# q loaded four tokens to a row, head halves on partition halves, in a retention and mixture-of-depths kernel

## Chip, cores and metric

The kernel runs on one core of one Trainium2 chip. The metric is the device time of one execution in microseconds: the median of several runs for the comparison, and one profiled run for the trace. The span of a trace is a little shorter than the time of a run (116.6 us of span in a profiled run of 118.38 us).

## What is computed

Two stages, the second on the output of the first. The reference, cut to what matters:

```python
# q, k, v: (4, 8, 768, 64) float32; x: (4, 768, 512)
def _attn_ref(q, k, v):
    gamma = 1.0 - 2.0 ** (-5.0 - np.arange(H))
    for t in range(S):
        state = gamma * state + einsum('bhd,bhe->bhde', k[:, :, t], v[:, :, t])
        y[:, :, t] = (1 / sqrt(D)) * einsum('bhd,bhde->bhe', q[:, :, t], state)

def _moe_ref(x, w_gate, w1, w2, capacity):          # x = y with the heads side by side
    scores = einsum('bsd,d->bs', x, w_gate)
    out = x.copy()
    for b in range(B):
        top_idx = argpartition(-scores[b], capacity)[:capacity]      # capacity = 128 of 768
        xe = x[b, top_idx]
        ye = maximum(xe @ w1, 0) @ w2                # 512 -> 1024 -> 512
        out[b, top_idx] = xe + sigmoid(scores[b, top_idx])[:, None] * ye
```

The kernel does the first stage in chunks. There are 12 tiles `j` (4 batches, 3 tiles of 256 tokens each). In a tile, the decay is put into q and k as factors (`gq`, `gk`), the products of q and k are masked and multiplied with v, and the state of all earlier tokens is added. The second stage needs the scores of all 768 tokens of a batch before it can rank them.

## The kernel before

All work is written as small functions, and a long string `ORDER` names them in the order in which they are put on the engines. Each engine takes its own instructions in that order. The names that the text uses: `l_q`, `l_k`, `l_v` load half a tile (j, half u), `l_wg` loads w_gate, `c_...` make constants, `warm` multiplies zeros, `cq` casts the first q tile, `ks` scales k, `tq` and `tk` transpose q and k on TensorE, `eq` and `ek` bring them to SBUF, `qk` and `mk` are the score product and its mask, `kv` and `se` add to the state and copy it, `qs` and `av` are the two products that make y, `ey`, `tx`, `ex` bring y to token order, `sp` and `esp` are the scores, `srt`, `esr`, `cp`, `cpi`, `dg`, `rk` rank them, `oh`, `gx`, `ga`, `gr` gather, `m1`, `rl`, `m2`, `cb` are the expert, `st` stores, and `sca` scatters.

The start of the order (cut):

```python
ORDER = (
    "c_tab;c_iota;l_k 0 1;c_zero;l_wg;c_small;l_q 0 1;l_q 0 0;l_k 0 0;l_v 0 0;c_mask;c_gq 0;l_v 0 1;c_ident;"
    "c_slg;c_szero;l_q 1 1;l_q 1 0;c_gk 1;l_k 1 1;cq 0 1;c_gq 1;c_wg;c_iota3;tq 0 1 S6;warm S0;l_k 1 0;l_v 1 0;"
    "eq 0 1 S6;warm S1;cq 0 0;c_gk 0;c_late;l_k 2 0;tq 0 0 S6;warm S2;l_v 1 1;c_gq 2;warm S3;l_k 2 1;ks 0 0;"
    "l_q 2 1;warm S4;eq 0 0 S6;ks 0 1;l_q 2 0;tk 0 0 S6;tq 1 2 S5;ek 0 0 S6;l_v 2 0;kv 0;eq 1 2 S5;tk 0 1 S6;"
    "l_k 4 1;qk 0 0 P0;ek 0 1 S6;mk 0 0 P0;l_v 3 0;se 0;qk 0 1 P1;..."
```

The functions that the change touches, and their neighbours:

```python
QX = many(NX, [128, H, 2, D], BF, "qx")     # NX = 7 buffers; KX and VX alike
QF = sb.tile([128, H, 2, D], FT)            # first q tile, float32; KF for k

def tok(src, j, u):                         # 128 rows of 2 tokens, 4 heads: 512 runs of 512 B
    b, jt = divmod(j, NJ)
    return bass.AP(tensor=src.tensor, offset=src.offset + b * H * S * D + jt * T * D + (u % 2) * 4 * S * D,
                   ap=[[2 * D, 128], [S * D, 8 if u == 2 else 4], [1, 2 * D]])

def load(x, src, j, u):                     # float32 in HBM, bf16 in SBUF
    h = slice(0, H) if u == 2 else slice(4 * u, 4 * u + 4)
    nc.gpsimd.dma_start(x[j % NX][:, h].rearrange("p h r d -> p h (r d)"), tok(src, j, u))

def l_q(j, u):
    if j:
        load(QX, q, j, u)
    else:
        nc.sync.dma_start(QF[:, 4 * u:4 * u + 4].rearrange("p h r d -> p h (r d)"), tok(q, j, u))

def l_wg():                                 # 512 elements of 4 B, one by one
    nc.sync.dma_start(wgf[:, :, 0], bass.AP(tensor=moe_w_gate.tensor, offset=moe_w_gate.offset,
                                            ap=[[1, 128], [128, HP]]))

def warm(bank):
    for _ in range(4):
        pe.matmul(PS[bank][:, :512], zero[:, :128], zero, start=True, stop=True)

def tq_(j, u, bank):
    for hp in range(HP)[hs(u)]:
        for r in range(2):
            for s in range(2):
                pe.transpose(tb(bank)[s * 64:(s + 1) * 64, hp, :, r, :], QX[j % NX][:, 2 * hp + s, r, :], ident)

def eq(j, u, bank):
    ve.tensor_mul(QT[j % 3][:, hs(u)]..., tb(bank)[:, hs(u)]..., gq[:, j % NJ, hs(u)]...)

def qk(j, u, bank):                         # weights: kT (64 x 64), moving: qT (64 x 128)
    for h in range(2):
        for r in range(2):
            for s in range(2):
                for c in range(2):
                    pe.matmul(p[c * 64:(c + 1) * 64, s, h, r, :], KT[...][...], QT[...][...], ...)

def ey(j, bank):                            # back to token order
    ac.activation(YT[j % 3].rearrange("p c h (i r) -> p (c h) i r", r=2),
                  PS[bank].rearrange("p (g r i) -> p g i r", g=2 * HP, r=2), AF.Copy)
```

## Time and profile before

| | before |
|---|---|
| time, median of 3 runs | 117.97 us (117.95 to 119.13) |
| span of the profiled run | 116.6 us |
| busy: TensorE (matmul), its weight loads | 93.6, 73.0 us |
| busy: DVE, ACT, POOL | 79.6, 73.5, 76.9 us |
| bytes moved by DMA | 19.69 MB in 44,003 packets |

The page gives the busy time of each engine, the span in 40 slices with a digit in tenths for each, the chain of work that ended last, the costliest groups of instructions, and the loads with the time from issue to landing. Some groups (engine, operation, out <- in, count, busy time and mean of one):

| group | count | busy us | mean ns |
|---|---|---|---|
| DVE mask `am <- pA, mask`, 128x1024 | 24 | 28.8 | 1219 |
| DVE `qT <- pA, gq`, 128x1024 | 10 | 6.9 | 685 |
| ACT `yT <- pA`, 128x1024 | 12 | 12.3 | 1022 |
| POOL issue of `vx`, `kx`, `qx` loads | 24, 22, 22 | 18.7, 17.5, 17.1 | 789, 799, 796 |
| TensorE transposes of q to `pA`, 128x128 out | 160 | 6.6 | 222 |

The mean of one TensorE instruction is its whole passage; instructions overlap, so the busy time of a group is far less than count times mean. A row of waits reads: who waited, for whom, microseconds in total, times, and the longest. A row of the stretches reads: from and to, length, then busy time and number of instructions of TensorE, its weight loads, DVE, ACT and POOL, then the granted clock, the share of the DMA engines (over 1 where packets overlap) and the GB/s written.

### The profile page before, as it was taken

What the parts mean: (1) busy time and instruction counts of PE and PEld (TensorE: products, weight loads), DVE (VectorE), ACT (ScalarE), POOL (GpSimd) and SP (SyncE); (2) the same over time, 40 slices, a digit from 0 to 9 for tenths busy, and PEclk for the clock granted to TensorE, in tenths of its full rate; (3) what the DMA queues carried; (4) which work ended last, traced back from release to release, by engine and by line L of the source; (5) the groups of instructions that cost most, each with busy time, mean ns of one, the idle gap of its engine ahead of it and who ended that gap; (6) DMA issues with size and microseconds to landing.
All of it is one profiled execution on the core that took longest, in us unless ns stands there. A gap on an engine that the chain in (4) does not pass through costs nothing.

```text
span 116.6 us, 4536 instructions
## 1 busy us (share of the span) xinstructions
PE 93.6 (80%) x1962; PEld 73.0 (63%) x1962; DVE 79.6 (68%) x218; ACT 73.5 (63%) x117; POOL 76.9 (66%) x129
## 2 busy tenths in 40 slices
PE   0089979998999888879988969898899999999000
PEld 0033557876777666669867757787789669884000
DVE  5295187983966999983794999969499795333000
ACT  7994279986698777836246949898687417143200
POOL 7999999989997998912999897870040060800800
PEclk9999999999999999985599999999999999999985
DMA  2999999999999999996999999999939007670270
GB/s 60 211 225 178 180 178 180 178 180 178 180 189 184 191 181 178 188 268 68 227 85 142 123 275 204 219 309 385 391 105 351 9 6 90 178 98 0 90 90 0
DMA packets 44003, 19.69 MB, mean 169 GB/s; under 512 B 36880, under 2 KB 39952, under 8 KB 43984
## 3 DMA queue, kind: packets, MB, share of 16 engines
q0 software_dynamic: 41344, 18.36, 114.5%
q1 hardware_dynamic: 2640, 1.05, 3.5%
q8 instruction: 15, 0.25, 0.8%
q14 instruction: 4, 0.03, 0.1%
HBM read 23.07 MB, written 7.34 MB: 261 GB/s over the span
## 4 chain that ended last, share of the span: by engine, by line
PE 62%; ACT 12%; issue 11%; DMA 6%; POOLq 2%; DVE 1%; POOL 1%; SPq 1%; ACTq 0%
PE pA L181 42%; PE pB L181 13%; PE pS L181 7%; ACT yT L181 4%; DMA QF<-in_q_dram 3%; ACT sst L181 3%; ACT kT L181 2%; DMA out_dram<-xs 2%; POOLq L645 2%; ACT xg L181 1%; POOL out_dram L595 1%; ACT xs L181 1%; DVE qT L181 1%; ACT ot L181 0%; SPq L277 0%
## 5 line engine op out<-in xcount | busy, mean ns | idle before, releaser
L181 DVE TENSOR_TENSOR am<-pA,mask 128x1024 bf16<-128x1024 f32 x24 | 28.8, 1219 | 3.7 <-PE pA L181 2.1
L589 POOL DMA_DIRECT2D out_dram<-xs x12 | 8.7, 722 | 16.4 <-ACT wr L181 8.2
L296 POOL DMA_DIRECT2D vx<-in_v_dram x24 | 18.7, 789 | 1.0 <-PE pA L181 0.5
L296 POOL DMA_DIRECT2D kx<-in_k_dram x22 | 17.5, 799 | 0.9 <-issue 0.3
L181 PEld LDWEIGHTS <-kp 64*128 64x128 bf16 (+1 forms) x256 | 14.9, 96 | 4.3 <-issue 0.8
L296 POOL DMA_DIRECT2D qx<-in_q_dram x22 | 17.1, 796 | 0.1
L181 ACT ACTIVATE sst<-pS 64x256 bf16<-64x256 f32 x40 | 15.0, 375 | 3.3 <-PE pS L181 2.5
L181 DVE TENSOR_SCALAR g<-wr,sc 128x256 bf16<-128x256 f32 (+4 forms) x44 | 15.9, 415 | 0.8 <-ACT wr L181 0.8
L181 ACT ACTIVATE yT<-pA 128x1024 bf16<-128x1024 f32 x12 | 12.3, 1022 | 4.7 <-PE pA L181 4.4
L595 POOL DMA_INDIRECT out_dram<-ot,idx x4 | 5.9, 1477 | 12.8 <-ACT ot L181 6.8
L181 PE MATMUL pS<-vx,kp 64*128 64x128 bf16 x160 | 12.3, 217 | 0.4 <-ACT sst L181 0.2
L181 PEld LDWEIGHTS <-qx 128*64 128x64 bf16 x192 | 6.0, 113 | 8.7 <-DVE qx L181 6.3
L181 PE MATMUL pA<-am,vx 64*64 64x128 bf16 x384 | 9.5, 220 | 2.1 <-issue 2.1
L181 PE MATMUL pA<-qT,kT 64*64 64x128 bf16 x384 | 9.8, 227 | 1.5 <-ACT kT L181 1.0
L181 ACT ACTIVATE kT<-pB 128x1024 bf16<-128x1024 bf16 (+1 forms) x8 | 7.3, 916 | 5.6 <-PE pB L181 5.5
L181 PEld LDWEIGHTS <-yT 128*128 128x128 bf16 x192 | 8.8, 99 | 3.1 <-ACT yT L181 2.4
L181 ACT ACTIVATE xs<-pA 128x1024 bf16<-128x1024 bf16 x10 | 10.2, 1022 | 0.9 <-PE pA L181 0.6
L181 DVE TENSOR_TENSOR qT<-pA,gq 128x1024 bf16<-128x1024 bf16 x10 | 6.9, 685 | 5.2 <-PE pA L181 5.2
L181 PEld LDWEIGHTS <-kT 64*64 64x64 bf16 x384 | 6.7, 110 | 3.7 <-ACT kT L181 2.0
L181 PEld LDWEIGHTS <-vx 64*64 64x64 bf16 x384 | 6.2, 106 | 3.8 <-issue 2.4
L181 DVE TENSOR_TENSOR kp<-kx,gk 128x512 bf16<-128x512 bf16 x22 | 8.3, 417 | 0.0
L181 PE MATMUL pA<-xg,w 128*128 128x128 bf16 x128 | 7.8, 219 | 0.0
(98 smaller groups left out, 172.0 us busy)
## 6 DMA issues: line engine op xcount, KB each, us to landing
out_dram<-xs POOLq DMA_DIRECT2D x12, 512.0 KB, 7.8
vx<-in_v_dram POOLq DMA_DIRECT2D x24, 128.0 KB, 5.4
qx<-in_q_dram POOLq DMA_DIRECT2D x22, 128.0 KB, 5.5
kx<-in_k_dram POOLq DMA_DIRECT2D x22, 128.0 KB, 5.6
w<-in_moe_w_dram POOLq DMA_DIRECT2D x8, 256.0 KB, 7.1
KF<-in_k_dram SPq DMA_DIRECT2D x2, 256.0 KB, 4.2
QF<-in_q_dram SPq DMA_DIRECT2D x2, 256.0 KB, 4.4
out_dram<-ot,idx POOLq DMA_INDIRECT x4, 4.8
```

The costliest lines, as they stand in the source:

```text
L181: i = getattr(self.engine, name)(*a, **k)
L296: nc.gpsimd.dma_start(x[j % NX][:, h].rearrange("p h r d -> p h (r d)"), tok(src, j, u))
L589: i = nc.gpsimd.dma_start(o, xs[:, 2 * j:2 * j + 2, :])
L595: i = nc.gpsimd.indirect_dma_start(out=out_rows, out_offset=bass.IndirectOffsetOnAxis(ap=IDX[b][:, :1], axis=0), in_=OT[b % 2], in_offset= ...
L645: with _tile.TileContext(nc) as tc:
```

## The change

Each q load now takes rows of four tokens (1 KB of float32, 512 B of bf16) instead of two. So that a load still covers four heads and 256 tokens, heads 0 to 3 lie on partitions 0 to 63 and heads 4 to 7 on partitions 64 to 127. A load has 256 runs instead of 512. The purpose is fewer and longer descriptors for q, to relieve the DMA queue and the engine that writes it. The queries of a tile then come out of the transposes in another order: (r, i) with token 4i + r, where it was 2i + r. The decay table, the mask and the copy back to token order follow that order. k and v keep two tokens to a row.

w_gate, 512 elements of 4 B each, goes to the end of the SyncE queue, behind k and q of the first tile; before it was second.

The order of all work was made anew for this: in particular the warm-up multiplications (16 instead of 20) stand ahead of all other TensorE work, the first state update follows them, and q of tile 0 is cast, transposed and evicted in one piece rather than two halves.

```diff
-    QX = many(NX, [128, H, 2, D], BF, "qx")
+    QX = many(NX, [128, 4, 4, D], BF, "qx")
-    QF = sb.tile([128, H, 2, D], FT)
+    QF = sb.tile([128, 4, 4, D], FT)
-    gq = sb.tile([128, NJ, HP, 2, 2, 64], BF)
+    gq = sb.tile([128, NJ, HP, 2, 4, 32], BF)
-    mask = sb.tile([128, 2, 2, 64], BF)
+    mask = sb.tile([128, 2, 4, 32], BF)
...
     def l_q(j, u):
-        if j:
-            load(QX, q, j, u)
-        else:
-            nc.sync.dma_start(QF[:, 4 * u:4 * u + 4].rearrange("p h r d -> p h (r d)"), tok(q, j, u))
+        o, jt = divmod(j, NJ)
+        src = bass.AP(tensor=q.tensor, offset=q.offset + o * H * S * D + jt * T * D + u * 4 * S * D,
+                      ap=[[4 * D, 64], [S * D, 4], [1, 4 * D]])
+        e, x = (nc.gpsimd, QX[j % NX]) if j else (nc.sync, QF)
+        e.dma_start(x[u * 64:(u + 1) * 64].rearrange("p h r d -> p h (r d)"), src)
...
-    def tq_(j, u, bank):
-        for hp in range(HP)[hs(u)]:
-            for r in range(2):
-                for s in range(2):
-                    pe.transpose(tb(bank)[s * 64:(s + 1) * 64, hp, :, r, :], QX[j % NX][:, 2 * hp + s, r, :], ident)
+    def tqb(bank):
+        return bf(bank).rearrange("p (u g c r i) -> p u g c r i", u=2, g=2, c=2, r=4)
+
+    def tq_(j, bank):
+        for h in range(4):
+            s = slice(h % 2 * 64, h % 2 * 64 + 64)
+            for r in range(4):
+                pe.transpose(tqb(bank)[s, :, h // 2, :, r, :], QX[j % NX][:, h, r, :], ident)
...
-    def eq(j, u, bank):
+    def eq(j, bank):
...
-      ... r=2),  PS[bank].rearrange("p (g r i) -> p g i r", g=2 * HP, r=2), AF.Copy)
+      ... r=4),  PS[bank].rearrange("p (g r i) -> p g i r", g=2 * HP, r=4), AF.Copy)
```

The start of the new order (the rest is cut; tiles 2 and 3 and tiles 8 and 9 overlap in other ways, and the order behind the last attention product differs in which expert comes first):

```diff
+    "c_small;c_tab;c_iota;l_k 0 0;l_q 0 1;l_k 0 1;l_v 0 0;c_slg;l_q 0 0;c_zero;c_szero;c_gk 0;l_q 1 1;warm S6;"
+    "c_ident;l_v 0 1;l_wg;c_gq 0;l_k 1 0;warm S6;l_k 1 1;l_v 1 0;c_gq 1;warm S6;c_iota3;ks 0 1;warm S6;l_q 1 0;"
+    "c_late;l_q 3 0;c_gq 2;l_k 2 1;l_v 1 1;ks 0 0;l_q 3 1;c_gk 1;cq 0;kv 0;l_q 2 1;c_wg;tq 0 S6;se 0;l_q 2 0;"
+    "tk 0 1 S0;tk 0 0 S1;l_k 2 0;ek 0 1 S0;eq 0 S6;ek 0 0 S1;l_k 3 0;ks 1 2;c_gk 2;qk 0 0 P1;l_v 2 1;c_mask;"
+    "qk 0 1 P2;tk 1 2 S6;mk 0 0 P1;l_v 2 0;tq 1 S0;ek 1 2 S6;l_k 3 1;mk 0 1 P2;qs 0 P1;kv 1;l_k 5 0;av 0 0 P1;..."
```

## The prediction

> **What bounds the kernel now.** I read the page first: busy times, the slices, the chain. From the slices, three lines, one digit for each 2.9 us:

> ```profile
> PE   0089979998999888879988969898899999999000
> ...
> PEclk9999999999999999985599999999999999999985
> DMA  2999999999999999996999999999939007670270
> ```

> TensorE is busy from about 6 us to 108 us, and DMA is full until about 60 us. The clock drops once in the middle (slices 18 to 20). The page's chain that ended last, by engine:

> ```profile
> PE 62%; ACT 12%; issue 11%; DMA 6%; POOLq 2%; DVE 1%; POOL 1%; SPq 1%; ACTq 0%
> ```

> So TensorE sets the end. Then the waits by engine, to see what TensorE still waits for and whether anybody waits for the loads that the change touches:

> ```profile
> PE pB L181 <- DVE qx L181: 6.3, 1, 6.3
> PE pA L181 <- issue: 3.4, 7, 0.9
> PE pA L181 <- ACT kT L181: 1.0, 2, 0.6
> DVE qx L181 <- DMA QF<-in_q_dram: 2.1, 1, 2.1
> ```

> The one long wait of TensorE is at the start, for the first q tile; its other waits for ACT and DVE add up to 3.7 us (ACT 1.0 + 0.9 + 0.8 + 0.6 + 0.2, DVE qT 0.2). After the first tile no compute engine waits for a transfer. The chain in order of time shows what the start is made of:

> ```profile
> 1.77 4.00 DMA QF<-in_q_dram
> ...
> 6.34 0.64 PE pB L181 x8
> 6.98 3.53 PE pA L181 x8
> 10.50 0.44 PE pB L181 x7
> 10.94 2.70 PE pA L181 x12
> ...
> 15.35 0.60 ACT kT L181
> ```

> The `pA` groups of 8 and 12 are the warm-up multiplications of zeros: 6.2 us of TensorE standing between the q transposes and the first k transposes. The first real score product (`qk 0`) starts at 15.24 us in the timeline, and by then only q of tiles 0 and 1, k of tile 0 and one state update are done. That stretch is where the new order can win. From there to `av 11`, the last attention product (88.8 us), the order is already dense; after it TensorE runs without a gap to 108 us.

> The last view is the GB/s row of the DMA answer for the first 12 us, 0.3 us per slice:

> ```profile
> GB/s 0 0 0 0 0 0 24 27 285 350 189 103 87 61 203 309 326 325 248 207 197 270 309 293 240 204 178 183 173 183 173 182 178 178 179 177 179 178 178 180
> ```

> The dip to 61 GB/s between 3.0 and 4.2 us is the w_gate transfer, 512 packets of 4 bytes, second in the SyncE queue. It landed 2.8 us after its issue at 1.23, so at 4.03.

> [...] Today every cast load of q, k and v writes 256 B rows (512 B read as fp32), and the trace has 36,880 of 44,003 packets under 512 B at a steady 178 to 180 GB/s written. The new q rows are 512 B. [...] the first eight warm-up multiplications take 3.59 us (0.45 each), the next twelve 2.76 us (0.23 each).

> **The change part by part.** *q loads, steady state.* 22 loads of 512 rows become 22 of 256. POOL's descriptor work goes by rows in the groups: 0.58 us for w1 (128 rows), 0.72 for w2 and stores (256), 0.79 for today's loads (512). I estimate 0.72 for the new ones, 22 x 0.07 = 1.5 us of POOL. It lies off the path: nobody waits for these loads. Worth 0 to 0.3 us.

> *Transposes and evictions.* A tile needs 16 q transposes before (4 pairs x 2 tokens x 2 heads) and after (4 head slots x 4 tokens), each 128x64 to 64x128. `eq` stays one 128x1024 multiply (0.68 us), `mk` 1.22 us, `ey` 1.02 us; only the order of columns within them changes. Sum 0. Four of 20 warm-up multiplications go.

> *w_gate behind the tile.* The dip is about (330 x 4 - 440) GB/s x 0.3 us = 264 KB, 0.8 us of first-tile traffic. q and k of tile 0 land up to 0.8 us earlier.

> *The start.* I replay it by hand with durations of the timeline. ACT first: table load and `first` end at 2.24; `gk 0` waits for `slg`, about 2.4, and takes 1.04 to 3.5; `gq 0`, `gq 1`, `gq 2` take 2.08 + 2.06 + 2.06 to 9.7; `gk 1` to 10.7; `se 0` 0.77 to 11.5; two half `ek 0` 0.60 each to 12.7. So `qk 0 0` starts near 12.8. DVE: constants to about 4; `ks 0 1` when its k lands (third in the queue, issued near 1.8, plus 3.1 to 4.0 us as the first k and the first q took), about 5.2 to 6.0; `c_late` 0.86 to about 7.1 (it waits for POOL's iota near 6.4); `ks 0 0` 0.75 to 7.9; `cq 0` about 1.0 to 1.4, to 9; `c_wg` 0.9, then `eq 0` 0.69 to 10.6, in time for 12.8. TensorE: 16 warm-ups from 3.0 (9 at 0.43, 7 at 0.22) to about 8.4; `kv 0`, `tq 0`, `tk 0` fit between 8.4 and 10.3. The first score product moves from 15.2 to 12.8, 2.4 us; the old order has then also transposed q of tile 1 (0.55), so the lead is about 1.9 us. Going on: `mk 0 0` 13.3 to 14.5, `mk 0 1` to 15.7, `av 0 1` done near 16.2 against 19.5 before (which has one more `kv`, 0.55: lead 2.75); `av 1` done near 20.3 against 24.0, where the old order is some 0.8 us of TensorE work further: lead near 2.8. At `qk 2` the same account gives about 2.5. I take **2.5 us**.

> *The rest.* The matmul work from there to the end is the same. In both lists what remains on TensorE behind `av 11` is the same sum: three expert first layers (about 1.95 each), four second layers (1.89 each), two rank sums (1.04 each), two gathers (1.50 each) and small ones, about 22 us. So the lead arrives at the end unless the new order waits more between. The old one has 3.7 us of dependency waits, and instruction gaps (0.3 to 0.9 us, no releaser) that should stay. I take 0 for the difference, plus or minus 1.5 us.

> Sum: 118.0 - 2.5 (start) - 0.2 (loads) + 0.5 (risk of a clock drop at the start, below) = 115.8; rounded for the gate's smaller share to **115.7 us**.

> **Rivals.** *The clock falls at the start.* After the warm-up the new order gives TensorE only some 1.7 us of work in 8.4 to 12.8. In the old trace 46 to 50 us, busy 3.20 of 4.00, was followed by this:

> ```profile
> 50.00:54.00 4.00, 3.45 (x86) 3.20 (x75) 2.21 (x9) 2.52 (x3) 0.00 (x0) 0.70 1.47 211
> 54.00:58.00 4.00, 4.00 (x60) 3.31 (x58) 2.91 (x5) 1.25 (x2) 3.04 (x6) 0.50 0.72 155
> ```

> The seventh figure is the clock. An emptier stretch may well do it again; tile 0 at half clock costs about 1 us, of which DVE's mask multiplications hide part. Time then 116.7. *The middle drop vanishes or comes twice.* TensorE does 60 instructions in 54 to 58 where 84 is usual, so a drop costs 2 to 3 us: 113.5 without, 118.5 with another. *ACT becomes the bound early.* It works from 2.4 to 20 us nearly without a pause in my replay, and one `ek` or `ey` behind an `se` moves everything: 116.5. *Loads arrive late.* The new order computes earlier from a queue that starts no earlier: `v 1 1` and `k 2 0` are issued near 9.3 and 12 and land some 5.4 us later (median of v), near 15 and 17.5; wanted near 19. Margin 2 us, unless 64-partition loads are slow. If they took 1.5 times as long, tiles 2 to 4 would wait and the time would be 119. The steady 0.73 us spacing against this. *The loads were the bound after all*, and fewer descriptors give more: [...] the waits speak against it.

> **Range and chances.** The start is worked out to about 1 us, the middle to 1.5 us, the clock to 1.5 us: together some 2.4 us for 8 in 10, a little more for the unreplayed 60 us in between. Range **112.5 to 118.8**. The 2% line lies at 115.6, almost on my number: faster by over 2% **0.47**, within **0.42**, slower by over 2% **0.11** (needs 120.3: late loads or two more clock drops).

> **What would show it.** Right: `qk 0` near 12.8 us, ACT being what it waits for; `av 11` near 86; the same gapless tail; no compute wait on q; POOL near 0.72 us per q load. Wrong: waits of DVE `kp` or TensorE on a transfer, a clock row with a drop near slice 4 or a second one later, dependency waits of TensorE well over 3.7 us, or a q transpose or `qT` eviction slower than 0.22 and 0.68 us.

## The result, and the profile after

In the first comparison the changed kernel takes 114.68 us (median of four runs, 113.19 to 117.55), the kernel before on the same chip 118.38 us (117.95 to 119.13). The ratio is 0.958, with a 95% interval of 0.950 to 0.966. Ratios leave disturbed executions out, and on this core few are left, so each is read beside the median of all executions.

One comparison is not enough here: executions of one and the same kernel differ by 3 to 6 us. The changed kernel was therefore measured twice more (e1 and e9 below). Over the three, its 14 executions have a mean of 115.57 us (two more on record for the first comparison, of 115.06 and 113.75 us, would make it 115.42), and 55 executions of the kernel before in the same comparisons 118.21 us: 2.6 us or 2.2% less. From the spread of these executions the difference is known to about 1.1 us either way, so that the kernel is faster is shown, and that it is so by over 2% is not: the interval of the first comparison is clear of 2%, those of e1 and e9 are not, and that of e1 includes 1. The prediction was 115.7 us from 118.0, 2.3 us less. Its range (112.5 to 118.8) held all three medians.

The profile after is of an execution of 115.92 us, span 114.1. Its slices (2.85 us each) and the chain by engine, from the page:

```profile
PE   0997799979898989795987979498999999999200
...
PEclk9999999999999999999679999976999999999965
DMA  2999999999999999999999999999206067520270
...
PE 47%; issue 16%; DVE 11%; ACT 8%; POOL 6%; DMA 5%; POOLq 2%; DVEq 0%; ACTq 0%
```

Two things differ from before. TensorE starts at 2.6 us, not 6.3. And the clock now drops twice (slices 20, 21 and 27, 28) where it dropped once; that execution is still faster. "issue", time in which an engine waited for nothing that the profile shows, has 16% of the chain where it had 11%.

Its first rows of the timeline of TensorE (start, length, what, and in brackets the idle time ahead with what ended it):

```profile
2.58 5.83 PE L181 MATMUL pB<-zero 128*128 128x512 bf16 x16 [2.58 <-DVE zero L248]
8.54 0.67 PE L181 MATMUL pS<-vx,kp 64*128 64x128 bf16 x4
9.75 0.38 PE L181 MATMUL pS<-vx,kp 64*128 64x128 bf16 x4 [0.54 <-DMA vx<-in_v_dram]
...
10.66 0.62 PE L181 MATMUL pA<-ident,kp 128*128 128x128 bf16 x8
12.23 0.64 PE L181 MATMUL pA<-qT,kT 64*64 64x128 bf16 x32 [0.95 <-ACT kT L181]
```

The first score product starts at 12.23 us (12.6 in e1's profile) against 15.24. The waits by engine, those of TensorE and the one long wait of a compute engine for a load:

```profile
DVE kp L181 <- DMA KF<-in_k_dram: 3.2, 1, 3.2
...
PE pB L181 <- DVE zero L248: 2.6, 1, 2.6
...
PE pA L181 <- issue: 2.5, 4, 1.4
...
PE pB L181 <- issue: 1.9, 2, 1.2
...
PE pA L181 <- ACT kT L181: 1.0, 1, 1.0
...
PE pS L181 <- DMA vx<-in_v_dram: 0.5, 1, 0.5
```

The 6.3 us that TensorE waited for the first q tile are gone. Its waits without a releaser ("issue") add up to 4.4 us where they were 3.9 (the 3.4 that the prediction shows and 0.5 for `pB`), and the longest is 1.4 us where it was 0.9. The chain in order of time says where they lie, and what the start hangs on now:

```profile
2.16 0.90 POOL vx L296
3.06 0.67 POOL qx L304
3.73 5.99 DMA vx<-in_v_dram
...
51.74 1.21 issue
...
71.42 1.44 issue
```

The first state update waits for v of tile 0, whose transfer takes 5.99 us; the chain goes over it, not over q. (In e9's profile it goes over k of tile 0, 5.28 us, instead.) The two gaps are followed by the two clock drops. The stretches of 4 us (busy time and instructions of TensorE, its weight loads, DVE, ACT and POOL, then clock, DMA share, GB/s written) show each gap and the drop behind it:

```profile
50.00:54.00 4.00, 2.79 (x85) 2.38 (x84) 3.03 (x7) 1.66 (x3) 3.62 (x6) 1.00 1.66 196
54.00:58.00 4.00, 4.00 (x52) 3.61 (x49) 4.00 (x8) 0.76 (x2) 3.48 (x7) 0.61 1.57 188
70.00:74.00 4.00, 2.56 (x66) 2.17 (x63) 2.63 (x7) 2.49 (x4) 2.68 (x5) 1.00 1.38 337
74.00:78.00 4.00, 4.00 (x74) 3.17 (x72) 2.96 (x4) 3.81 (x6) 1.55 (x4) 0.67 1.45 402
```

From the last attention product (ended 86.6 us, before 88.8) to the end of the span are 27.5 us, before 27.8: the tail is the same.

The GB/s row of the first 12 us after, 0.3 us for each slice:

```profile
GB/s 0 0 0 0 0 0 148 87 292 307 217 355 309 196 251 265 208 156 202 245 256 231 216 192 138 88 94 109 109 141 133 149 138 156 163 175 168 183 183 182
```

The dip of w_gate has moved from 3.0 to 4.2 us to 7.5 to 8.7 us, behind k and q of the first tile. Its lowest slice is 88 GB/s, where it was 61, with less traffic around it, and w_gate itself lands 5.9 us after its issue instead of 2.8.

### The profile page after: what moved, and what is told of

It reads as the page before. It is cut to its first block, busy times and chain, and to the rows that moved or that the text cites. A ratio compares the mean times of both kernels' runs of the same rounds, so it can differ in the third digit from the quotient of the medians.

```text
span 114.1 us, 4540 instructions
## 1 busy us (share of the span) xinstructions
PE 94.0 (82%) x1958; PEld 73.4 (64%) x1958; DVE 79.9 (70%) x216; ACT 74.0 (65%) x117; POOL 74.6 (65%) x128
## 2 busy tenths in 40 slices
DMA packets 37859, 19.69 MB, mean 172 GB/s; under 512 B 25616, under 2 KB 33808, under 8 KB 37840
## 4 chain that ended last, share of the span: by engine, by line
PE 47%; issue 16%; DVE 11%; ACT 8%; POOL 6%; DMA 5%; POOLq 2%; DVEq 0%; ACTq 0%
PE pA L181 27%; PE pB L181 11%; PE pS L181 9%; DMA vx<-in_v_dram 5%; DVE am L181 5%; POOL out_dram L598 4%; DVE g L181 3%; ACT kT L181 3%; DVE qT L181 2%; ACT xs L181 2%; POOLq L648 2%; ACT yT L181 1%; ACT ht L181 1%; POOL vx L296 1%; ACT sst L181 1%
## 5 line engine op out<-in xcount | busy, mean ns | idle before, releaser
L181 DVE TENSOR_TENSOR am<-pA,mask 128x1024 bf16<-128x1024 f32 x24 | 28.8, 1219 | 3.9 <-PE pA L181 2.9
L181 ACT ACTIVATE sst<-pS 64x256 bf16<-64x256 f32 x40 | 15.0, 375 | 9.4 <-PE pS L181 6.9
L181 PEld LDWEIGHTS <-kp 64*128 64x128 bf16 (+1 forms) x256 | 15.4, 98 | 6.4 <-issue 2.4
L296 POOL DMA_DIRECT2D kx<-in_k_dram x22 | 16.7, 765 | 1.7 <-DMA kx<-in_k_dram 0.8
L181 DVE TENSOR_SCALAR g<-wr,sc 128x256 bf16<-128x256 f32 (+4 forms) x44 | 16.6, 446 | 0.0
L304 POOL DMA_DIRECT2D qx<-in_q_dram x22 | 14.0, 637 | 2.0 <-DMA vx<-in_v_dram 0.8
L181 ACT ACTIVATE yT<-pA 128x1024 bf16<-128x1024 f32 x12 | 12.2, 1022 | 3.3 <-issue 1.8
L181 PE MATMUL pS<-vx,kp 64*128 64x128 bf16 x160 | 13.2, 221 | 1.0 <-DMA vx<-in_v_dram 0.5
L181 ACT ACTIVATE xs<-pA 128x1024 bf16<-128x1024 bf16 x9 | 9.2, 1024 | 4.3 <-PE pA L181 4.1
L181 PE MATMUL pA<-qT,kT 64*64 64x128 bf16 x384 | 9.5, 224 | 2.0 <-ACT kT L181 1.0
L181 PEld LDWEIGHTS <-yT 128*128 128x128 bf16 x192 | 8.7, 97 | 2.5 <-ACT yT L181 0.9
L181 PE MATMUL pA<-am,vx 64*64 64x128 bf16 x384 | 8.6, 224 | 0.9 <-issue 0.9
L181 PEld LDWEIGHTS <-kT 64*64 64x64 bf16 x384 | 6.4, 108 | 4.1 <-issue 1.8
L181 DVE TENSOR_TENSOR kp<-kx,gk 128x512 bf16<-128x512 bf16 x22 | 8.2, 419 | 0.1
L181 PE MATMUL pB<-zero 128*128 128x512 bf16 x16 | 5.8, 545 | 2.6 <-DVE zero L248 2.6
L181 PEld LDWEIGHTS <-vx 64*64 64x64 bf16 x384 | 6.2, 108 | 2.5 <-issue 1.3
L181 PE MATMUL pA<-xg,w 128*128 128x128 bf16 x128 | 7.8, 219 | 0.0
L181 ACT ACTIVATE kT<-pB 128x1024 bf16<-128x1024 bf16 x6 | 6.1, 1022 | 2.5 <-PE pB L181 2.4
L181 PEld LDWEIGHTS <-w 128*128 128x128 bf16 x128 | 7.3, 98 | 0.3
```

The costliest lines, as they stand in the source:

```text
L181: i = getattr(self.engine, name)(*a, **k)
L304: e.dma_start(x[u * 64:(u + 1) * 64].rearrange("p h r d -> p h (r d)"), src)
```

## Experiments

e1 to e4 ran on one chip with 40 runs of the kernel before (median 118.06 us, mean 118.19). e5 to e8 shared 8 (117.70), e9 to e11 shared 11 (117.77), e12 had 11 (116.92).

**e1, the changed kernel again.** No edit.

> The changed kernel once more, for a second profile and as the yardstick of this chip. Both theories: 113 to 114.5 us against about 118.3 for the kernel before. The theory of the clock (part of the gain is that the clock drops once or not at all where the first profile had two drops after 54 and after 74 us): a faster profile shows fewer or shorter drops and lacks TensorE gaps of over 1 us ahead of them; the first profile's two drops and its 114.1 us of span belong together.

Measured: 115.22 us, median of 4 (113.45 to 116.72), ratio 0.989 [0.974, 1.004]. The profiled execution was the quickest (113.45), with the same start and a single clock drop, of one slice. So the two drops of the first profile are no fixture of the change. Nor does each gap bring a drop: the one of 1.34 us that ends at 76.77 us has none behind it, and the drop (69.6 to 73.0) stands behind a gap of 0.78.

**e2, the layout alone.** The new q rows, masks and tables in the order of before; the halves of `cq`, `tq`, `eq` of tile 0 become one.

```diff
- ...cq 0 1;...tq 0 1 S6;...eq 0 1 S6;...cq 0 0;...tq 0 0 S6;...eq 0 0 S6;...
+ ...cq 0;...tq 0 S6;...eq 0 S6;...          (with the QX, gq, mask, l_q, tq_, eq, ey of the changed kernel)
```

> New q layout and loads in the OLD order (only the two half casts, half transposes and half evictions of q of tile 0 become whole ones, at the place of the second half). Order theory (the gain is the new start and a denser order; nobody waits for q): within 1 us of the kernel before, 117.3 to 118.8. Load theory (256 longer descriptors instead of 512 relieve the queue and POOL, and that carries the gain): 114.5 to 116. Either way POOL's time per q load falls from 0.79 to about 0.63.

As the first half of q of tile 0 is now done with the second, two of the five warm-up groups come to stand ahead of all q transposes; this run is not the layout alone in that.

Measured: 117.21 us, median of 20 (mean 117.33), ratio 0.984 [0.977, 0.991]; first score product at 15.4 us, as before.

**e3, the order alone.** The new order with the q layout of before.

```diff
- QX = many(NX, [128, 4, 4, D], BF, "qx")   (and gq, mask, l_q, tq_, eq, ey of the changed kernel)
+ QX = many(NX, [128, H, 2, D], BF, "qx")   (and those of the kernel before)
```

> New order with the OLD q layout (rows of two tokens on 128 partitions, 512 descriptors a load, queries in order (r, i) of two). Order theory: 113 to 114.5, as the changed kernel, since no engine waited for q. Load theory: 116.5 to 118, with waits on loads that the changed kernel has not, because the queue then serves later what the new order asks for earlier.

Measured: 114.47 us, median of 4 (113.54 to 115.57), ratio 0.977 [0.957, 0.997]. The groups of POOL's q loads in e2 (new layout) and e3 (old layout):

```profile
L303 POOL DMA_DIRECT2D qx<-in_q_dram x22 | 13.8, 639 | 0.6 <-issue 0.5
```

```profile
L295 POOL DMA_DIRECT2D qx<-in_q_dram x22 | 16.8, 773 | 0.0
```

The new rows cost POOL 0.13 us less for each load, 3 us over all, whatever the order. With the new order this buys nothing that could be seen: e3, without the new rows, was no slower than e1 (114.47 and 115.22, same chip, four executions each). With the old order the new rows gave 0.85 us (20 and 40 executions). Where those 0.85 us come from isn't located: no wait for a q load went away, for there was none in steady state.

**e4, the kernel before with its warm-ups first.** Nothing else is changed.

```diff
- ...c_iota3;tq 0 1 S6;warm S0;...;warm S1;...;warm S2;...;warm S3;...;warm S4;...
+ ...c_iota3;warm S0;warm S1;warm S2;warm S3;warm S4;tq 0 1 S6;...
```

> The kernel before with one edit: its five groups of warm-up multiplications stand together ahead of the first q transposes instead of between them and the first k transposes. Theory that the warm-ups on TensorE's path made the late start: the first score product moves from 15.2 to about 13.5 us (then the decay table of k and its scaling on DVE hold it) and the time falls by 1 to 1.7 us, to 116.6 to 117.3. Rival, that ACT's tables and DVE's order hold the start anyway: under 0.4 us of gain.

Measured: the first score product moves from 15.24 to 12.83 us, 2.4 us as the prediction had it for the new order, with five warm-up groups moved. But the time is 117.19 us, median of 20, ratio 0.986 [0.979, 0.993]: 0.9 us of the 2.4 arrive. The timeline and the stretches of its profile show a loss near the end. Timeline of TensorE:

```profile
84.77 0.91 PE L180 MATMUL pA<-xg,w 128*128 128x128 bf16 x7 [2.59 <-issue]
```

Stretches:

```profile
82.00:86.00 4.00, 1.41 (x17) 1.29 (x13) 4.00 (x14) 0.29 (x1) 0.51 (x2) 0.81 1.14 315
86.00:90.00 4.00, 4.00 (x78) 3.47 (x78) 0.27 (x3) 2.12 (x3) 0.00 (x0) 0.76 0.01 3
```

TensorE stood for 2.59 us with nothing to wait for, and ran at half clock from 84.5 to 87.9 us. This gap moved the question from the start to the gaps.

The profile is not typical of e4, though. Its execution had a mean granted clock of 0.969, and 18 of the 20 had less than 0.95 (mean of all 0.932), where 36 of the 40 of the kernel before had 0.95 or more (mean 0.964). As the clock falls to half in the traces (granted 0.50 from 51.6 to 58.5 us in the kernel before), a mean 0.032 lower than before over 115 us is some 7 us more at half clock (an estimate from these means), and that is enough to take the missing 1.5 us. Where the clock fell in those executions can't be seen, for none was profiled. TensorE is nearly empty at the start of e4 (1.71 us of work from 8 to 12 us), so a fall there is a rival to the late gap, and it is untested.

**e5, w_gate last in the queue, in the kernel before.**

```diff
- c_tab;c_iota;l_k 0 1;c_zero;l_wg;c_small;l_q 0 1;l_q 0 0;l_k 0 0;l_v 0 0;...
+ c_tab;c_iota;l_k 0 1;c_zero;c_small;l_q 0 1;l_q 0 0;l_k 0 0;l_wg;l_v 0 0;...
```

> The kernel before with w_gate moved behind k and q of tile 0 in the SyncE queue, nothing else. Order theory (this start waits for its own program order and the warm-ups, not for the transfer): first q lands about 0.5 to 1 us earlier than at 5.78, the first q transposes start that much earlier, but the first score product stays within 0.7 us of 15.2 and the time within 0.7 us of the kernel before. Rival (the chain of before runs through that q transfer, so it is worth its whole 0.8 us): 0.8 us faster.

Measured: 120.53 us, median of 4 (118.02 to 121.56), ratio 1.032 [1.023, 1.042]. q is cast at 4.83 us, 1 us earlier than the 5.80 of before, as the prediction's 0.8 us for the dip would have it. But DVE then has a new wait:

```profile
DVE wg L282 <- DMA wgf<-in_moe_w_gate_dram: 3.8, 1, 3.8
```

The casts of w_gate (`c_wg`) stand in DVE's order ahead of the first `eq`. w_gate now lands at 9.3 us, and everything behind it on DVE stands still. So the early q is lost again, and the first score product starts at 15.74 us, 0.5 us later than before. The move of the load can only pay together with a later `c_wg`, which the new order has (behind `cq 0`; the cast starts at 9.50 us there, without a wait).

The wait doesn't explain the median. In this profile, of the quickest of the four executions, the 0.5 us are made good by tile 5 (its `ey` ends at 46.2 us, before 46.6), and the span is 116.2 us, not above the 116.6 of before. Why the other three took 119.9 us and more isn't shown.

**e6, w_gate second in the queue, in the changed kernel.**

```diff
- ...l_k 0 0;l_q 0 1;l_k 0 1;l_v 0 0;c_slg;l_q 0 0;...;l_v 0 1;l_wg;...
+ ...l_k 0 0;l_wg;l_q 0 1;l_k 0 1;l_v 0 0;c_slg;l_q 0 0;...;l_v 0 1;...
```

> The changed kernel with w_gate back in second place. In the profile of the changed kernel DVE waits 3.2 us for k of tile 0 and TensorE 0.5 us for v. Transfer theory: the 512 packets of 4 bytes delay k by about 0.8 us, the first score product moves from 12.2 to about 13, and the time rises by 0.5 to 1 us. Rival (the landing of v, 9.7 us, sets the start): the first score product within 0.3 us and the time the same.

Measured: 115.46 us, median of 4 (115.06 to 115.73), ratio 0.987 [0.983, 0.991]. The first k that DVE waits for comes at 8.27 us instead of 6.63 (7.4 and 7.5 in the other two profiles of the changed kernel), and the first score product starts at 13.8. Yet the time is that of the changed kernel in its own comparisons: no difference can be measured. The clock was half from 11 to 18 us and again from 66 to 73; the one long gap without a releaser is of 1.0 us, ahead of 65.8.

**e7, a start of my own.** The new order with the first 15 us arranged again: the k transposes ahead of q's, the state update, `c_mask`, `c_late` and `gq 2` elsewhere.

```diff
- ...;cq 0;kv 0;l_q 2 1;c_wg;tq 0 S6;se 0;l_q 2 0;tk 0 1 S0;tk 0 0 S1;...
+ ...;cq 0;l_q 2 1;l_q 2 0;tk 0 1 S0;tk 0 0 S1;tq 0 S6;kv 0;l_k 2 0;...
```

> The changed kernel with its first 15 us put in another order: second half of v of tile 0 ahead of q of tile 1; k transposes ahead of q transposes and the state update behind both; the decay tables of later tiles behind the first k evictions on ACT; mask made early; first mask multiplication ahead of the scaling of k of tile 1. Start theory (what is won at the first tiles arrives at the end): first score product near 10.7 instead of 12.2 us and 0.7 to 1.2 us off the time. Rival (the next tiles are held by ACT and by landings, the start is slack): no gain, the second tile at the same time as before.

Measured: the first score product comes at 11.7 us, the earliest of all, and the time is 118.73 us, median of 4, about 3 us more than the changed kernel. Its clock row and the stretches:

```profile
PEclk9999855558999999999999999855999999999965
```

```profile
10.00:14.00 4.00, 2.04 (x57) 1.63 (x57) 2.65 (x5) 1.89 (x4) 3.52 (x6) 0.96 1.68 182
14.00:18.00 4.00, 3.95 (x56) 3.09 (x59) 2.88 (x8) 1.40 (x2) 4.00 (x6) 0.50 1.63 188
```

TensorE was busy for 2.04 us of 4, and then had half its clock until 27 us. In the changed kernel's first profile the same stretch has 3.05 us of work, and the clock stayed. This is the rival "the clock falls at the start", in a start that is quicker and emptier. That the emptiness brought it about is argued: in e8, which has the order of the changed kernel, the clock fell at 12.2 us, and in e10, with 2.50 us of work in the same stretch, it stayed.

**e8, the changed kernel without the loads of tiles 8 to 11.** Those tiles then compute with the data that lies in their buffers; all compute instructions stay.

```diff
- ...l_k 8 0;...l_v 9 0;...l_q 8 0;...   (24 loads: q, k and v of tiles 8 to 11)
```

> The changed kernel without the loads of q, k and v of tiles 8 to 11 (their buffers keep the data of earlier tiles, so this part of the output is of other data; all compute work stays). It asks what the gaps of TensorE without a releaser are. Theory of the full queue: they stand at every 256th instruction of TensorE[...]; with a third of the loads gone, DMA is free from about 40 to 60 us, the gaps there vanish, the clock drop that follows them too, and the time falls by 1 to 3 us, to 112 to 114, with a smaller spread. Rival (gaps come from something else on TensorE): same gaps, time within 0.5 us of the changed kernel.

Measured: 112.07 us, median of 4 (111.86 to 112.74), ratio 0.959 [0.954, 0.964]. It lost about 2 us at the start by a clock drop (12 to 19 us), and won them back and more: after that the clock did not drop until TensorE was through, and TensorE's waits without a releaser were these two:

```profile
PE pA L178 <- issue: 0.6, 1, 0.6
...
PE pB L178 <- issue: 0.4, 1, 0.4
```

**e9, the changed kernel once more.** No edit, beside e10 and e11 on the same chip.

> The changed kernel unaltered, as the yardstick on the same chip for the two below: median 114.5 to 115.5 us, spread of 3 to 4 us between its runs.

Measured: 115.78 us, median of 6 (113.41 to 119.05), ratio 0.976 [0.968, 0.984]. Its profile has a gap of TensorE of 2.4 us that ends at 78.6 us, in the burst of stores. The waits put it down to the eviction `qT`, which ended 0.7 us earlier (77.92) and which the product behind the gap, `am` by `vx`, does not read.

**e10, the changed kernel without its twelve stores.** The scatters stay; the rows that no expert takes are not written.

```diff
- ...st 2;...st 4;...st 3;...st 6;...st 0;...st 7;...st 1;...st 8;...st 9;...st 5;...st 10;...st 11;...
```

> The changed kernel without its twelve plain stores of the first stage (the output then holds only the scattered rows; all compute and all loads stay). Theory of the full queue[...]: the longest gaps without a releaser, those between 70 and 85 us where stores are issued in bursts, vanish; gaps before 65 us, under the loads, stay; time 1 to 2 us below the changed kernel. Rival (the gaps come from the loads or from TensorE alone): within 0.5 us.

Measured: 111.02 us, median of 6 (108.04 to 115.96), ratio 0.922 [0.916, 0.929]: 4.8 us less than e9. Stretches of its profile, to be read beside those of 70 to 78 us above:

```profile
70.00:74.00 4.00, 4.00 (x111) 3.41 (x108) 3.70 (x7) 3.94 (x7) 0.00 (x0) 1.00 0.03 6
74.00:78.00 4.00, 4.00 (x115) 3.50 (x113) 3.45 (x8) 3.52 (x7) 0.00 (x0) 1.00 0.01 4
```

With no transfers TensorE does 226 products in these 8 us, at full clock and without a gap; with 337 to 402 GB/s it did 140. Nobody on TensorE waits for a store, so the 4.8 us are not a wait that the profile names. The removal also takes 8.7 us of work from POOL, so this run alone doesn't say whether it is the transfers or POOL's work; e8 likewise takes both. One gap at least needs no work of POOL beside it. In e1's profile POOL did nothing in the stretch that holds the gap of 1.34 us:

```profile
74.00:78.00 4.00, 2.66 (x64) 2.20 (x65) 3.01 (x6) 1.58 (x2) 0.01 (x1) 1.00 1.47 409
```

**e11, loads spaced.** A small `iota` (128x32) on POOL behind each load of tiles 2 to 11.

```diff
+ def pace(j):
+     if j >= 2:
+         nc.gpsimd.iota(pad, pattern=[[1, 32]], base=0, **iota)
```

> The changed kernel with a short POOL instruction (about 0.14 us, a 128x32 iota on a scratch tile) behind every load of q, k and v from tile 2 on, so that a load starts every 0.87 us instead of 0.73 and DMA is not kept full. No compute is changed. Theory of the full queue: time from issue to landing falls from 5.6 to under 4 us, the gaps of TensorE under the loads become shorter, and the time falls by 0.5 to 1.5 us if the last v tile still lands in time (the loads end some 7 us later). Rival (the loads have no slack): waits of DVE and TensorE on transfers appear and the time rises by 1 to 3 us.

Measured: 115.24 us, median of 6 (113.96 to 116.39), ratio 0.975 [0.969, 0.981], the same as e9. The rate between 10 and 40 us fell from about 183 to between 150 and 172 GB/s, q loads landed 5.0 us after issue instead of 5.8, and no engine began to wait for a load. The clock dropped at 11 to 17 and 63 to 71 us. Less crowding of this size does not help, or what it gives went to the clock: inconclusive.

**e12, stores later.** Meant to beat both kernels: four of the twelve stores leave the burst at 66 to 78 us.

```diff
- ...qs 8 P2;st 6;...av 9 0 P0;st 7;...ek 10 2 S2;st 8;...tk 11 2 S3;st 9;...
+ ...st 10;st 6;st 7;...sca 1;st 8;...sca 0;st 9;...
```

> The changed kernel with the same twelve stores, but four of them moved later: those of tiles 6 and 7 behind that of tile 10 (about 83 us instead of 66 to 70), those of tiles 8 and 9 behind the first two scatters (about 96 us instead of 75 to 78). Theory of the full queues[...]: the written rate at 66 to 80 us falls from 330-400 GB/s to under 250, the gaps without a releaser between 70 and 80 us shrink from 1.4-2.6 to under 0.7 us, and the time falls by 1 to 3 us against the changed kernel (115.3 over its three comparisons), to 112.5-114.5. Rivals: the late stores stand ahead of the last two scatters on POOL and in the DMA queues, and the end waits for them, or the gaps only move behind 83 us: 115 to 118, not faster than the changed kernel. Or the removed stores of the earlier experiment gained by POOL's time alone: then nothing changes, 115.

Measured: 114.73 us, median of 6 (111.61 to 116.54); the kernel before took 116.92 on that chip. That is 2.2 us less than before, as for the changed kernel. No ratio with an interval is on record. The profiled execution was the quickest of the six:

```profile
66.00:70.00 4.00, 3.10 (x80) 2.80 (x79) 3.25 (x11) 2.96 (x5) 3.06 (x10) 1.00 1.40 202
70.00:74.00 4.00, 4.00 (x76) 3.16 (x74) 2.89 (x4) 3.64 (x6) 0.00 (x0) 0.68 1.40 368
74.00:78.00 4.00, 4.00 (x108) 3.34 (x106) 2.84 (x8) 2.19 (x4) 0.00 (x0) 0.89 0.21 56
```

The full rate ends near 74 us instead of 79, and the gap that stood behind it (71 to 79 us in the changed kernel) is gone. But the gap of 0.9 us ahead of 69 us stayed, with a clock drop behind it. Of 14 executions of the changed kernel none was under 113.19 us; two of these six were (111.61 and 112.25), in a comparison in which the kernel before was also some 1.2 us quicker. The theory's 112.5 to 114.5 was not met by the median; a gain over the changed kernel is not shown.

### The gaps, from the traces

The gaps without a releaser of over 0.3 us that were looked at stand behind one kind of transfer, that of the instruction queue. The page has this queue alike in all kernels:

```profile
q8 instruction: 15, 0.25, 0.8%
```

That is 15 packets, 0.25 MB, so 16 KB each. TensorE has 3,916 matmuls and weight loads in the changed kernel, and 3,916 / 256 = 15.3. Numbered in the trace, with the semaphore instructions of its queue, the instructions at which it resumes lie a multiple of 256 apart. Some of them, with the start and length of the packet ahead (us):

```
kernel   instruction   packet          resumes at   packet's end to resume
before   704           24.64 + 0.94    26.91        1.33
changed  1984          50.67 + 0.89    52.95        1.39
changed  2752          70.60 + 0.98    72.86        1.28
e1       3008          74.51 + 1.01    76.77        1.25
e9       3008          76.23 + 1.01    78.61        1.37
e3       3264          78.52 + 1.01    80.95        1.42
e4       3264          82.41 + 1.02    84.77        1.34
```

2752 - 1984 = 3 x 256; 3008 and 3264 are one and two blocks further. TensorE resumes 1.25 to 1.42 us behind the packet's end in these seven, and 1.2 to 1.6 us in the ten gaps of over 0.3 us that the first two profiles have at such places. The packets there take 0.9 to 1.0 us whether the gap is 0.3 or 1.4 (1.02 ahead of e4's 2.59); what differs is how late they start. Most boundaries have no gap: in the changed kernel's first profile 4 of 15 have one of over 0.3 us. In the 4 us up to the instruction at which TensorE resumes, the DMA share is 1.23 to 1.81 in those ten, at 179 to 385 GB/s. Where less is moved, boundaries pass without one: in the changed kernel those with packets at 80.75, 84.74, 90.69 and 98.46 us (share 0.02 to 0.66 from 2 us ahead of the packet to its end), and all between 70 and 82 us in e10 (0.01 to 0.03). Much traffic doesn't always bring one: the kernel before passes the boundary with the packet at 88.76 us (share 1.16, 326 GB/s) without a gap. So in this case a boundary of 256 instructions costs 0.3 to 2.6 us for some of the blocks, in stretches in which the DMA engines are full.

That each packet brings TensorE its next 256 instructions is inferred from the queue's name, the count and the positions; that it waits behind data transfers is argued from position, packet and traffic. What held the packet's start back can't be seen in the trace.

The end of `ey` (y to SBUF, one for each tile) in the profiled executions splits the time:

```
kernel   tile 0   tile 5   tile 11   tile 5 to 11
before   21.3     46.6     89.9      43.3
e2       21.4     46.6     89.3      42.7
e4       18.8     44.2     88.6      44.4
changed  16.8     44.8     87.7      42.9
e1       17.2     45.0     85.1      40.1
e9       17.2     44.7     88.2      43.5
e3       17.2     43.9     83.4      39.5
e12      17.2     44.7     83.5      38.8
e7       19.7     50.0     90.9      40.9
e10      17.6     46.7     83.1      36.4
e8       19.4     46.4     83.2      36.8
```

Up to tile 5 the changed kernel has the same time in its three profiles, to 0.4 us. Behind it the same instructions take 40.1 to 43.5 us, and in e8, with fewer transfers, 36.8. So the differences between executions of the changed kernel arise in the second half, and 3.3 to 6.7 us lie there between it and e8, which has the same compute instructions.

## Why the prediction was right, and where it was not

**Time and bound.** 115.7 predicted; 114.68, 115.22 and 115.78 measured. Faster by over 2% had 0.47, against 0.42 for the same: 2.2% less over all, almost on the line, as the text said. That no steady-state load is waited for stood in the waits, and e3 bears it out: the order without the new q rows was no slower.

**The start: right in what moved, too small by half a microsecond.** First score product at 12.23 to 12.6 us instead of 12.8, so 2.7 to 3.0 us earlier instead of 2.4. e4 shows the named cause by itself: the same 2.4 us by moving the warm-ups alone. ACT is what the product waits for in the timeline (0.95 us for `kT`), as said, but the tables on ACT, through by 10.2 us, were not what held it. The chain goes over v of tile 0: landed 9.72, then the update, the transposes (to 11.3), `ek`. The replay had given v no time of its own, and it had k at 5.2 to 6.0 us, which came at 6.63 (7.4 and 7.5 in e9 and e1).

**"So the lead arrives at the end unless the new order waits more between": this step was weak.** At tile 5 the lead is still 1.8 us (46.6 to 44.8; e1 1.6, e9 1.9). Whether it arrives is decided behind tile 5. In e4, where the order behind is as before, 0.9 of 2.4 us arrived. In e3, with the new order and the old rows, 3.6 us arrived. So some 2.7 us (3.6 - 0.9, same chip, four executions for e3) lie between the warm-ups moved alone and the whole new order, where the prediction had 0 plus or minus 1.5. Part of them may be clock that e4 lost (mean 0.932, e3 0.958) and not work that the new order saved. Two errors of opposite sign nearly cancelled: less of the lead lasted than predicted, and more came in the second half. That the sum came out so close was luck. Which piece of the order does it was not tried and stays open.

**"Instruction gaps (0.3 to 0.9 us, no releaser) that should stay": wrong in size.** They are up to 2.4 us in the changed kernel and 2.6 in e4, they stand only where much is being transferred, and they move with the order. Removing transfers, and the work of POOL that issues them, was worth about 3 us (e8) and 4.8 us (e10), more than the whole change. This is the largest term of the time that the sum did not have. That it makes the difference between the two kernels isn't shown: in the first profiles the gaps add up to 4.4 and 3.9 us.

**The clock.** The rivals had "vanishes" at 113.5 and "comes twice" at 118.5. Both happened to one kernel: one short drop in an execution of 113.45 us, two drops in one of 115.92. In the traces a drop is to half clock for 3.4 us (54.9 to 58.3 and 75.3 to 78.8 us in the changed kernel's first profile), for about twice that (51.6 to 58.5 us before), and in e7 from 13.7 to 27.4 us. So one of the first two lengths can take up to 1.7 or 3.4 us (an estimate, half of its length), which fits the 2 to 3 us that the prediction took. How often it comes varies from execution to execution: the mean clock of the 16 executions of the changed kernel on record goes from 0.904 to 0.982, and their times follow it (113.41 us at 0.982, 119.05 at 0.904; correlation -0.90). The order has a part in it all the same, with means of 0.949 for the changed kernel, 0.932 for e4, 0.902 for e7 and 0.966 for 70 executions of the kernel before. The fall at the start, taken at +0.5 us of risk, did not come in the changed kernel's three profiles. It came with the same start in e8 and nearly the same in e6 and e11, where `ey 0` ended at 18.8 to 20.1 us instead of 16.8 to 17.2. Part of this is a later first score product (12.8 to 13.8 us); from there to the end of `ey 0` it was 6.0 to 6.6 us instead of 4.6 to 4.9, so the fall cost 1.0 to 2.0 us where 1 was predicted. In e7 it came in full. What makes the clock fall is not shown. In the changed kernel's first profile the stretches ahead of the drops had no idle time over 1.44 us, and TensorE was busy for 64 to 70% of the 4 us (2.56 and 2.79). Short idle time is not enough by itself: e2 had a gap of 2.40 us to 86.36 us, in a stretch with 1.95 us of work, and no drop behind it.

**Loads.** POOL's time for one q load was put at 0.72 us, from the rows of 256; it is 0.64, so 22 loads save 3.1 us of POOL's busy time (17.1 to 14.0) and not 1.5. It lies off the path, as said. Packets went from 44,003 to 37,859, those under 512 B from 36,880 to 25,616, and the steady rate from 178 to 180 to about 183 GB/s: 2%. The rival of slow 64-partition loads fell: q lands 5.6 us after issue, k on 128 partitions 5.6 as well. In the time the layout is worth nothing visible under the new order and 0.85 us under the old, where 0.2 was predicted.

**w_gate.** e5 confirms the size of the dip for q (1 us earlier), and shows what the step left out: the reader of w_gate had to move too. Without that the first score product comes 0.5 us later instead of earlier; e5's 2.8 us are more than that, and not explained. In the changed kernel the move brings the first k 0.8 to 1.6 us earlier (e6) and no time that could be measured.

**The tail** is the same, as the account of the remaining work had it.

## What to carry to other kernels

When a load is moved back in a queue, look for its reader in the order of every engine: a small cast that stands ahead of critical work turns a free move into a stall. Gaps of TensorE without a releaser deserve a look at their spacing in instructions and at the traffic at that time; if they come at a fixed spacing (here multiples of 256 instructions) and vanish where next to nothing is transferred (4 to 6 GB/s in e10), suspect the traffic before looking for a dependency. Less traffic helped here (e8, e10); spreading it (e11, e12) was not shown to. Look also at the granted clock of all executions, not only of the profiled one: e4's profile was the exception. Measure a change of 2% with many executions of both kernels: single profiles of one kernel differed here by as much as the change.
